# Attention and two MLPs with Strassen products: three weight steps a batch in attention, VectorE's queue filled up to TensorE's clock, and two output chunks in turns at two borders

## The chip, the cores and the metric

The kernel runs on one core of one Trainium2 chip. The metric is the device time of one execution in microseconds; the time before is the median of three runs. The profile is one further execution, recorded by the hardware profiler; its times count from the start of the recorded span.

## The reference

Three stages follow each other. Everything is fp32, on 896 tokens (2 batches of 448), 12 heads of 64, and a width of 768.

```python
scores = scale * np.matmul(q, k.transpose(0, 1, 3, 2)) - np.log(S)
attn = 1.0 / (1.0 + np.exp(-scores))
x = np.matmul(attn, v)                  # -> (896, 768)
# first MLP: 768 -> 1536 -> 768
rms = np.sqrt(np.mean(x * x, axis=-1, keepdims=True) + 1e-06)
xn = x / rms * rms_g
g = xn @ w_gate
x = g * (1.0 / (1.0 + np.exp(-g))) * (xn @ w_val) @ w_out
# second MLP: 768 -> 2048 -> 768
h = x @ w_in
out = h * (1.0 / (1.0 + np.exp(-h))) @ w_out2
```

## The kernel before

**Precision.** A product in fp32 is made of three passes on TensorE: each operand is split into a high part, rounded by ScalarE (`high`, L109), and a low part, the difference, taken by VectorE (`low`, L112); high by high, high by low and low by high are summed in PSUM. One matmul is 128x128 by 448 columns.

**Weights.** All weights come as 68 slabs of 128x768. Each goes through two raw buffers, three float tiles and a ring of four split tiles. The halves are these: `front` (Prelu on ScalarE L122, a shift on VectorE L125, a combining step on VectorE L127, and then the next slab's load, L106, on the queue of SP), and `back_std` (high, then low) or, for a Strassen product, `back_mac` (four more sums on VectorE, and four pairs of high and low). `step()` advances this stream by one instruction or two. So a slab's load is issued only when the slab two ahead of it has been combined at L127, and the loads of keys (`load_pair`, L378) and values are on the same queue, in program order.

**Order.** Nothing reorders: every engine runs its instructions as the program wrote them. What is written when is set by a small planner: `clock["pe"]` and `clock["dve"]` sum up costs of TensorE and VectorE as the code goes, and after each piece of TensorE's work `pump()` calls `step()` as long as VectorE's clock stays half a microsecond (`MARGIN`) below TensorE's. A second list, `fore`, holds sums and splits of activations, which takes turns with the weights. A product that needs a weight tile that isn't there yet calls `step()` until it is.

**Stages.** Attention works on 12 pairs of heads in chunks of 112 rows, three chunks a batch (48 chunks, 16 batches): the scores of a batch (L407, ScalarE's sigmoid L415), then the value products of the batch before (L423). After each batch two weight steps are taken, while the batch before was of the pairs 1 to 6 (L539 to L543). The keys of pair i are split by VectorE (`prep`, L392) when pair i-1 starts. After attention come the opening products (L553 to L567): two gate chunks and two value chunks (g and v) of batch 0, while batch 1 is normalised, then the same for batch 1 (L615), then the value products v of p = 1 and, for p = 1 to 5, `strassen` g1 to g5 with a value product between. Each `strassen` (L302) is seven groups of nine matmuls on three PSUM banks (x, y, z), named A11, S1, S2, A12, S3, S4, A22 after their weights; ScalarE saves three of the partial results, VectorE adds three, ScalarE ends with silu (L344 to L348). The o stage multiplies the hidden vector h by the output weights, six chunks of 12 tiles; the i stage is one plain product and the seven strassens i1 to i7 with the result g, and the e stage multiplies g by the last weights, six chunks of 16 tiles, with a copy on VectorE (L742) and a store for each chunk. Before e the eight tiles of g are split (ghi by ScalarE, glo by VectorE, each in two halves of 896); these are the `fore` work of i7 and of the first e chunk.

Of the kernel before, what the change touches and what calls it, by code (L numbers as in the profile page):

```python
# [8 lines left out]
F32 = mybir.dt.float32  # L9
F32R = mybir.dt.float32r  # L10
U32 = mybir.dt.uint32
I32 = mybir.dt.int32
AF = mybir.ActivationFunctionType
# [3 lines left out]
B, H, S, D = 2, 12, 448, 64  # L17
NP = H // 2
DM = H * D
FF1, FF2 = 1536, 2048  # L20
P = 128
CP = 112
NC = S // CP
KD, K1, K2 = DM // P, FF1 // P, FF2 // P
SLAB = 6 * P
HALF = 3 * P
NT = B * S
EPS = 1e-6
BATCH = 3
MARGIN = 0.5  # L30
RING = 4
PASSES = ((0, 0), (0, 1), (1, 0))
ORDER = (0, 2, 4, 1, 3, 5)
# [3 lines left out]
def tile_attention_two_mlps(  # L37
# [27 lines left out]
    nc = tc.nc  # L65
# [7 lines left out]
    rp = ctx.enter_context(tc.tile_pool(name="rp", bufs=1))  # L73
# [13 lines left out]
    for p in range(1, K1 // 2):  # L87
        pair = [("mac", 4 * p), ("std", 4 * p + 2), ("std", 4 * p + 3)]
        items += pair if p > 1 else pair[1:] + pair[:1]
    first = 2 * K1  # L90
# [7 lines left out]
    order = [t for kind, s in items for t in ((s, s + 1) if kind == "mac" else (s,))]  # L98
# [9 lines left out]
    def high(dst, src):  # L108
        nc.scalar.activation(dst, src, AF.Copy)  # L109

    def low(dst, src, hi):
        nc.vector.tensor_tensor(dst, src, hi.bitcast(F32), ALU.subtract)  # L112
# [118 lines left out]
    fore, turn = [], [True]  # L231
    clock = {"pe": 0.0, "dve": 0.0}

    def step():

        if head[0] is None:
            head[0] = next(steps, StopIteration)
        can = head[0] is not None and head[0] is not StopIteration
        if fore and not (can and turn[0]):
            turn[0] = True  # L240
            cost, do = fore.pop(0)
            clock["dve"] += cost
            do()
            return True
        turn[0] = False
        if not can:
            return False
        clock["dve"] += head[0]
        head[0] = next(steps, StopIteration)
        return True  # L250

    def pump():
        clock["dve"] = max(clock["dve"], clock["pe"] - 3.0)
        while True:
            ahead = [c for c in (fore[0][0] if fore else None, head[0]) if c not in (None, StopIteration)]
            if ahead and clock["dve"] + min(ahead) > clock["pe"] - MARGIN:
                return
            if not step():
                return

    def evac(cost):
        clock["dve"] = max(clock["dve"], clock["pe"]) + cost

    def until(ready):
        while not ready():
            assert step()

    def weights(s):
        until(lambda: s in wt)
        return wt[s]  # L270

    def done(s, n=1):
        live["ring"] -= n
        del wt[s]


    def product(ps, tiles, acts, bs, last=True, after=None):

        n = len(tiles)
        ps = ps if isinstance(ps, list) else [ps[:, b, :S] for b in range(2)]  # L280
        for i, (w, a) in enumerate(zip(tiles, acts)):
            s, o = divmod(w, 6)
            until(lambda: a in act)
            t, x = weights(s)[:, :, o * P : (o + 1) * P], act[a]
            for step_, (jw, jx) in enumerate(PASSES):
                for b in bs:
                    nc.tensor.matmul(  # L287
                        ps[b],
                        t[:, jw],
                        x(jx)[:, b * S : (b + 1) * S],  # L290
                        start=(i == 0 and step_ == 0),
                        stop=(i == n - 1 and step_ == 2),
                    )
            clock["pe"] += 0.2027 * 3 * len(bs)
            if last and o == 5:
                done(s)
            if after:
                after(i)
            if not lead:
                pump()  # L300

    def strassen(name, s, forms, dst, after=None):  # L302

# [54 lines left out]
    act = {("x", k): (lambda j, k=k: x[k][:, j]) for k in range(KD)}  # L358
# [4 lines left out]
    with ExitStack() as actx:  # L363
# [10 lines left out]
        def load_pair(i):  # L374
            b, hp = pairs[i]
            kq[i] = ap.tile([P, 2, S], F32, tag="kq", name=f"kq{i}", bufs=3)
            if i:
                nc.sync.dma_start(kq[i], kqd[b, hp])  # L378
            else:
                for j in range(2):  # L380
                    nc.sync.dma_start(kq[i][:, j], kqd[b, hp, :, j])
# [122 lines left out]
        n = len(pairs)  # L504
# [12 lines left out]
        seen, ready = 0, []  # L517
        chunks = [(i, c) for i in range(n) for c in range(NC)]
        batches = [chunks[j : j + BATCH] for j in range(0, len(chunks), BATCH)]
        for before, batch in zip([[]] + batches, batches + [[]]):  # L520
            for i, c in batch:
                if c == 0:
                    if i + 1 < n:
                        prep(i + 1)
                    if i + 2 < n:
                        load_pair(i + 2)
                        load_v(i + 2)
                    if i == 0:
                        load_next()
                    if i == 2:  # L530
                        load_next()
                scores(i, c)
            while ready:
                collect(ready.pop(0))
            for i, c in before:
                attend(i, c)
                if c == NC - 1:
                    ready.append(i)
            for _ in range(2):  # L539
                if 0 < seen <= NP:  # L540
                    step()
                if seen > NP:
                    next(normal, None)  # L543
            seen = batch[-1][0] if batch else n
# [17 lines left out]
        r = npool.tile([P, S], F32, tag="r", name="r1")  # L562
# [8 lines left out]
    fp = ctx.enter_context(tc.tile_pool(name="fp", bufs=1, reuse_waits="tile"))  # L571

    def sums_of(name, r, t):

        (b11, b21), (b12, b22) = [[r[:, b, j] for j in range(2)] for b in range(2)]
        tt = nc.vector.tensor_tensor
        todo = [
            (0.62, lambda: tt(b11, b12, b11, ALU.subtract)),
            (0.62, lambda: tt(b12, b22, b12, ALU.subtract)),
            (0.62, lambda: tt(b22, b22, b11, ALU.subtract)),  # L580
            (0.62, lambda: tt(b21, b21, b22, ALU.subtract)),
        ]
        return todo
# [29 lines left out]
    f = [fp.tile([P, 2, NT], F32, tag=f"F{p}", name=f"h{p}") for p in range(K1 // 2)]  # L613
    xs6 = [("x", k) for k in ORDER]
    for n in range(4):  # L615
        product(opening[n], range(6 * n, 6 * n + 6), xs6, (1,))
        m = n % 2
# [32 lines left out]
    for p in range(1, NP1):  # L650
        final = p == NP1 - 1
# [6 lines left out]
        for m in range(2):  # L658
            ps = ps_tile(f"v{p}_{m}")
            s = 4 * p + 2 + m  # L660

            def after(i):
                if final and m == 1 and i in (1, 3):
                    free = [f"x{ORDER[j]}" for j in (i - 1, i)]
                    fore.extend(halve("h", 3 + i // 2, f[3 + i // 2], xp, free[0], xp, free[1]))
# [12 lines left out]
    w0 = 6 * 2 * K1  # L678
    x2 = {}
    r2 = [rp.tile([P, 2, 2, S], F32, tag=f"r{t}", name=f"yr{t}") for t in range(3)]  # L680
    for m in range(KD):
        ps = ps_tile(f"o{m}")

        def after(i):
            if m == KD - 1 and i in (3, 7):
                fore.extend(halves_of("y", r2[i // 4], i // 4))

        product(ps, range(w0, w0 + K1), [("h", k) for k in range(K1)], (0, 1), after=after)
        w0 += K1
        x2[m] = fp.tile([P, 2, NT], F32R, tag=f"F{m}", name=f"y{m}")  # L690
        v = x2[m].rearrange("p j (b s) -> p j b s", b=2)
        high(v[:, 0], ps[:, :, :S])
        low(v[:, 1], ps[:, :, :S], v[:, 0])
        evac(1.09)
        nc.scalar.activation(r2[m // 2][:, :, m % 2], ps[:, :, :S], AF.Copy)
        act["y", m] = lambda j, m=m: x2[m][:, j]
        if m % 2:
            fore.extend(sums_of("y", r2[m // 2], m // 2))
    fore.extend(halves_of("y", r2[2], 2))


# [8 lines left out]
    for p in range(NP2):  # L710
        pool, tag = (xp, f"x{p}") if p < 6 else (rp, f"r{p - 6}")
# [3 lines left out]
        s = w0 // 6  # L715
        if p == 0:
            for m in range(2):
                ps = ps_tile(f"i{m}")
# [14 lines left out]
    for q, (ht, lt) in enumerate(((0, 1), (2, 3)), 6):  # L733
        fore.extend(halve("g", q, g2[q], xp, f"x{ht}", xp, f"x{lt}"))

    for m in range(KD):
        for bs in ((0, 1),) if m < KD - 1 else ((0,), (1,)):
            ps = ps_tile(f"e{m}_{bs[0]}")
            product(ps, range(w0, w0 + K2), [("g", k) for k in range(K2)], bs, bs[-1] == 1)
            sl = slice(bs[0], bs[-1] + 1)  # L740
            o = rp.tile([P, 2, S], F32, tag=f"r{(2, 0, 1)[m % 3]}" if m < 5 else f"r{(1, 2)[bs[0]]}", name=f"out{m}_{bs[0]}")
            nc.vector.tensor_copy(o[:, sl], ps[:, sl, :S])  # L742
            evac(1.09)
            nc.sync.dma_start(out[m * P : (m + 1) * P, sl], o[:, sl])
        w0 += K2


def _slabs(w, nk, order=None):

    import numpy as np  # L750

    k, m = w.shape
    t = np.ascontiguousarray(w).view(np.int64).reshape(nk, P, m // P, P)
    t = t.transpose(2, 0, 1, 3)
    return t if order is None else t[:, list(order)]
# [36 lines left out]
```

## Time and profile before

| what | value |
|---|---|
| three runs | 599.11, 602.41, 605.66 us, median 602.41 |
| profiled execution | 599.66 us, its span 597.9 us |
| mean granted clock of TensorE in it | 0.982 of full speed |
| TensorE busy | 564.7 us, 94% of the span |
| VectorE busy | 350.0 us, 59% |
| ScalarE busy | 277.8 us, 46% |

The span is what the profile shows between first and last instruction; 1.76 us of the profiled execution lie around it. TensorE is busy nearly throughout, so time is lost or gained where it stands still or runs at the lower clock.

### The profile page before, as it was taken

What the parts mean: (1) busy time and instruction counts of PE and PEld (TensorE: products, weight loads), DVE (VectorE), ACT (ScalarE), POOL (GpSimd) and SP (SyncE); (2) the same over time, 40 slices, a digit from 0 to 9 for tenths busy, and PEclk for the clock granted to TensorE, in tenths of its full rate; (3) what the DMA queues carried; (4) which work ended last, traced back from release to release, by engine and by line L of the source; (5) the groups of instructions that cost most, each with busy time, mean ns of one, the idle gap of its engine ahead of it and who ended that gap; (6) DMA issues with size and microseconds to landing.
All of it is one profiled execution on the core that took longest, in us unless ns stands there. A gap on an engine that the chain in (4) does not pass through costs nothing.

```text
span 597.9 us, 7040 instructions
## 1 busy us (share of the span) xinstructions
PE 564.7 (94%) x2840; PEld 484.6 (81%) x2840; DVE 350.0 (59%) x503; ACT 277.8 (46%) x366; POOL 0.2 (0%) x4
## 2 busy tenths in 40 slices
PE   6999994999899999999999999998888979999997
PEld 4545564998799999999999999987777758999996
DVE  3557649496577674696444566666665794434200
ACT  5887834444345362664333445455456672222100
POOL 0000000000000000000000000000000000000000
PEclk9999996999899999999999999999898999999999
DMA  8645002141144342343333313313331244432000
GB/s 254 231 146 188 6 0 97 62 148 64 53 159 160 129 148 93 106 159 106 127 111 116 116 61 106 105 54 105 104 107 53 103 162 137 165 130 84 31 32 31
DMA packets 14512, 64.99 MB, mean 109 GB/s; under 512 B 1872, under 2 KB 2384, under 8 KB 14480
## 3 DMA queue, kind: packets, MB, share of 16 engines
q1 hardware_dynamic: 14480, 64.55, 32.7%
q8 instruction: 22, 0.36, 0.3%
q14 instruction: 10, 0.08, 0.0%
HBM read 61.79 MB, written 2.75 MB: 108 GB/s over the span
## 4 chain that ended last, share of the span: by engine, by line
PE 89%; DVE 7%; ACT 2%; DMA 0%; issue 0%; SPq 0%; DVEq 0%; ACTq 0%
PE e L287 17%; PE v L287 15%; PE o L287 15%; PE av L423 6%; PE sc L407 6%; PE g L287 3%; PE i L287 2%; DVE glo L112 2%; DVE w L112 2%; PE g2x L312 1%; PE i5x L312 1%; PE g4x L312 1%; PE i2x L312 1%; PE i1x L312 1%; PE g3x L312 1%; PE g5x L312 1%
## 5 line engine op out<-in xcount | busy, mean ns | idle before, releaser
L112 DVE TENSOR_TENSOR w<-f,w 128x768 fp32r<-128x768 f32 (+1 forms) x80 | 70.7, 894 | 109.3 <-ACT w L109 109.3
L109 ACT ACTIVATE w<-f 128x768 fp32r<-128x768 f32 (+1 forms) x80 | 63.0, 793 | 125.4 <-PE e L287 56.5
L287 PE MATMUL v<-x,w 128*128 128x448 f32 x432 | 91.4, 373 | 8.0 <-DVE w L112 8.0
L287 PE MATMUL e<-ghi,w 128*128 128x448 f32 x384 | 96.4, 366 | 0.0
L287 PEld LDWEIGHTS v<-x,w 128*128 128x128 f32 x432 | 83.1, 193 | 15.4 <-DVE w L112 8.4
L287 PEld LDWEIGHTS e<-ghi,w 128*128 128x128 f32 x384 | 72.1, 188 | 6.0 <-DVE w L112 0.4
L127 DVE SCALAR_TENSOR_TENSOR f<-f,raw 128x768 uint32<-128x768 uint32 x68 | 64.9, 955 | 13.7 <-ACT f L122 10.6
L122 ACT ACTIVATE f<-raw 128x768 f32<-128x768 f32 x68 | 61.4, 904 | 21.5 <-DMA raw<-in_w 17.2
L287 PE MATMUL o<-hhi,w 128*128 128x448 f32 x288 | 70.3, 366 | 0.0
L287 PE MATMUL e<-glo,w 128*128 128x448 f32 x192 | 58.1, 370 | 5.9 <-DVE glo L112 5.9
L287 PEld LDWEIGHTS o<-hhi,w 128*128 128x128 f32 x288 | 54.1, 188 | 4.2
L415 ACT ACTIVATE a<-sc,logs 112x896 f32<-112x896 f32 x48 | 45.0, 1004 | 10.4 <-PE sc L407 10.0
L287 PEld LDWEIGHTS e<-glo,w 128*128 128x128 f32 x192 | 35.4, 188 | 11.8 <-DVE glo L112 9.3
L287 PE MATMUL o<-hlo,w 128*128 128x448 f32 x144 | 40.9, 366 | 0.0
L407 PEld LDWEIGHTS sc<-ks 64*112 64x112 f32 x288 | 26.0, 184 | 17.7 <-ACT ks L396 4.5
L407 PE MATMUL sc<-ks 64*112 64x448 f32 x288 | 35.9, 394 | 4.5 <-ACT ks L396 4.5
L423 PE MATMUL av<-a,vr 112*64 112x448 f32 x192 | 39.6, 548 | 0.0
L125 DVE TENSOR_SCALAR raw<-raw 128x768 uint32<-128x768 uint32 x68 | 37.7, 554 | 2.4 <-DMA raw<-in_w 2.4
L423 PEld LDWEIGHTS av<-a,vr 112*64 112x64 f32 x192 | 12.4, 136 | 20.4 <-issue 18.3
L287 PEld LDWEIGHTS o<-hlo,w 128*128 128x128 f32 x144 | 27.1, 188 | 2.1
L742 DVE COPY out<-e 128x896 f32<-128x896 f32 (+1 forms) x7 | 6.7, 956 | 28.5 <-PE e L287 28.5
L112 DVE TENSOR_TENSOR glo<-g,ghi 128x896 fp32r<-128x896 f32 x16 | 17.0, 1082 | 3.8 <-ACT ghi L109 3.8
(252 smaller groups left out, 681.3 us busy)
## 6 DMA issues: line engine op xcount, KB each, us to landing
raw<-in_w SPq DMA_DIRECT2D x68, 768.0 KB, 4.3
kq<-in_kq SPq DMA_DIRECT2D x11, 448.0 KB, 6.4
vr<-in_v SPq DMA_DIRECT2D x12, 224.0 KB, 5.4
out_t<-out SPq DMA_DIRECT2D x5, 448.0 KB, 2.5
kq<-in_kq SPq DMA_DIRECT2D x2, 224.0 KB, 2.7
out_t<-out SPq DMA_DIRECT2D x2, 224.0 KB, 1.9
eye<-in_eye SPq DMA_DIRECT2D x1, 49.0 KB, 6.4
g_sb<-in_g SPq DMA_DIRECT2D x1, 3.0 KB, 6.6
```

What stands on the lines that cost most here:

```text
L109: nc.scalar.activation(dst, src, AF.Copy)
L112: nc.vector.tensor_tensor(dst, src, hi.bitcast(F32), ALU.subtract)
L122: nc.scalar.activation(f, words[:, :, 1].bitcast(F32), AF.Prelu, scale=2.0**-112, alpha=2.0**32)
L125: nc.vector.tensor_scalar(z, z, 29, None, ALU.logical_shift_right)
L127: nc.vector.scalar_tensor_tensor(fu, fu, 3, z, ALU.logical_shift_left, ALU.bitwise_or)
L287: nc.tensor.matmul(ps[b], t[:, jw], x(jx)[:, b * S : (b + 1) * S], start=(i == 0 and step_ == 0), stop=(i == n - 1 and step_ == 2),)
L312: nc.tensor.matmul(ps, w[a][:, jw, t * P : (t + 1) * P], forms(b, t, jx), start=(start and t == 0 and n == 0), stop=(stop and t == 2 and n ...
L407: nc.tensor.matmul(ps[:CP, h, :S], ks[i][rows, jk, 0, c * CP : (c + 1) * CP], ks[i][rows, jq, 1, :], start=(step == 0), stop=(step == 2),)
L415: nc.scalar.activation(a, ps[:CP, :, :S], AF.Sigmoid, bias=logs[:CP], scale=D**-0.5)
L423: nc.tensor.matmul(ps[h * D : (h + 1) * D], vr[i][:, c, h, :], a[:, h, :], start=(c == 0), stop=(c == NC - 1),)
L742: nc.vector.tensor_copy(o[:, sl], ps[:, sl, :S])
```

## The change

There are three parts. `pump()` loses its half microsecond: steps are now written as long as VectorE's clock stays at or below TensorE's. In attention three weight steps are taken after a batch in place of two (while the batch before was of pair 6, two). And a new function `duo` runs the first two output chunks of o and of e in turns, two weight tiles (two k) for chunk 0 and then two for chunk 1, the second chunk in two single PSUM banks; the host lays the weight tiles out in that order. The results of these two chunks are taken out after both, in halves of 448 columns for each batch where they were 896 (`collected` for o, `put` for e).

```diff
-            if ahead and clock["dve"] + min(ahead) > clock["pe"] - MARGIN:
+            if ahead and clock["dve"] + min(ahead) > clock["pe"]:
...
-    def product(ps, tiles, acts, bs, last=True, after=None):
+    def product(ps, tiles, acts, bs, last=True, after=None, first=True, final=True):
...
-                        start=(i == 0 and step_ == 0),
-                        stop=(i == n - 1 and step_ == 2),
+                        start=(first and i == 0 and step_ == 0),
+                        stop=(final and i == n - 1 and step_ == 2),
...
+    def duo(name, w, nk, key):
+
+        pair = [ps_tile(f"{name}0"), [bank(f"{name}1_{b}") for b in range(2)]]
+        for k in range(0, nk, 2):
+            for ps in pair:
+                product(ps, (w, w + 1), [(key, k), (key, k + 1)], (0, 1), first=k == 0, final=k == nk - 2)
+                w += 2
+        return [[pair[0][:, b, :S] for b in range(2)], pair[1]]
...
-            for _ in range(2):
-                if 0 < seen <= NP:
+            for j in range(3):
+                if 0 < seen <= NP - (j > 1):
                     step()
+                if j > 1:
+                    break
...
+    pair = duo("o", w0, K1, "h")
+    w0 += 2 * K1
+    for m in range(2):
+        collected(m, pair[m], [(slice(b, b + 1), pair[m][b].rearrange("p (a s) -> p a s", a=1)) for b in range(2)])
+    for m in range(2, KD):
...
+    pair = duo("e", w0, K2, "g")
+    w0 += 2 * K2
+    for m in range(2):
+        for b in range(2):
+            put(m, b, 1, pair[m][b].rearrange("p (a s) -> p a s", a=1))
+    for m in range(2, KD):
```

How instructions move is seen at three places. In the rows, the line comes first, then the operation, and out<-in; lines of the kernel after are its own.

The first is SP's queue in attention, before. `raw3` is the load of weight slab 3 (the slabs are used in the order 0, 1, 2, 3, 6, 7, 4), `kq6` the load of the keys and queries of pair 6, `vr6` its values.

```order
L385 DMA vr5_300<-in_v 112x512
L378 DMA kq6_354<-in_kq 128x896
L385 DMA vr6_356<-in_v 112x512
L106 DMA raw3_389<-in_w 128x1536
L378 DMA kq7_412<-in_kq 128x896
L385 DMA vr7_414<-in_v 112x512
L378 DMA kq8_479<-in_kq 128x896
L385 DMA vr8_481<-in_v 112x512
L106 DMA raw6_521<-in_w 128x1536
L378 DMA kq9_537<-in_kq 128x896
L385 DMA vr9_539<-in_v 112x512
```

And after:

```order
L393 DMA vr5_303<-in_v 112x512
L105 DMA raw3_344<-in_w 128x1536
L386 DMA kq6_360<-in_kq 128x896
L393 DMA vr6_362<-in_v 112x512
L386 DMA kq7_418<-in_kq 128x896
L393 DMA vr7_420<-in_v 112x512
L105 DMA raw6_439<-in_w 128x1536
L105 DMA raw7_486<-in_w 128x1536
L386 DMA kq8_491<-in_kq 128x896
L393 DMA vr8_493<-in_v 112x512
L386 DMA kq9_549<-in_kq 128x896
```

The load of raw3 now stands ahead of kq6 and not ahead of kq7, raw6 and raw7 stand ahead of kq8 (and, below the rows printed, raw4 ahead of kq10).

The second is VectorE's queue behind the normalisation of batch 1 (the opening products), before. `x4` and `x5` are the last normalised tiles, `w2` and `w3` split weights, `f3` a float tile; L578 is a sum of activations for the first strassen.

```order
L112 TENSOR_TENSOR x5_89<-xr2_92,x5_89 128x448
L112 TENSOR_TENSOR w2_570<-f2_432,w2_570 128x768
L127 SCALAR_TENSOR_TENSOR f3_523<-f3_523,raw3_389 128x768
L125 TENSOR_SCALAR raw6_521<-raw6_521 128x768
L112 TENSOR_TENSOR w3_982<-f3_523,w3_982 128x768
L578 TENSOR_TENSOR xr0_90<-xr0_90 128x448
L127 SCALAR_TENSOR_TENSOR f6_980<-f6_980,raw6_521 128x768
```

And after, where L588 is the same sum:

```order
L111 TENSOR_TENSOR x5_89<-xr2_92,x5_89 128x448
L588 TENSOR_TENSOR xr0_90<-xr0_90 128x448
L589 TENSOR_TENSOR xr0_90<-xr0_90 128x448
L124 TENSOR_SCALAR raw7_486<-raw7_486 128x768
L590 TENSOR_TENSOR xr0_90<-xr0_90 128x448
L591 TENSOR_TENSOR xr0_90<-xr0_90 128x448
L126 SCALAR_TENSOR_TENSOR f7_1035<-f7_1035,raw7_486 128x768
L111 TENSOR_TENSOR w6_1050<-f6_532,w6_1050 128x768
```

The steps of w2, f3 and w3 are no longer there (they stand in attention), and the sums and w6 follow the normalisation at once.

The third is ScalarE's queue at the border from strassen i2 to i3, before. L332 is the last save of i2, L344 to L348 its silu, `w42_0` to `w42_3` are the weight tiles of i3.

```order
L332 ACTIVATE i2s2_3007<-i2x_3002 128x448
L109 ACTIVATE w42_0_3067<-f42_2885 128x768
L344 ACTIVATE g2_2_3001<-g2_2_3001 128x448
L347 ACTIVATE g2_2_3001<-g2_2_3001 128x896
L348 ACTIVATE g2_2_3001<-i2x_3002 128x448
L109 ACTIVATE w42_1_3112<-s42_3050 128x768
L109 ACTIVATE w42_2_3114<-f43_3022 128x768
L109 ACTIVATE w42_3_3117<-f42_2885 128x384
```

And after, where L340 is the save and L352 to L356 are the silu:

```order
L108 ACTIVATE w42_0_3064<-f42_2892 128x768
L340 ACTIVATE i2s2_3018<-i2x_3013 128x448
L108 ACTIVATE w42_1_3079<-s42_3047 128x768
L108 ACTIVATE w42_2_3091<-f43_3029 128x768
L352 ACTIVATE g2_2_3012<-g2_2_3012 128x448
L108 ACTIVATE w42_3_3115<-f42_2892 128x384
L355 ACTIVATE g2_2_3012<-g2_2_3012 128x896
L356 ACTIVATE g2_2_3012<-i2x_3013 128x448
```

The high parts of w42_1, w42_2 and w42_3 now stand ahead of the last silu, where they stood behind it.

## Rows read from the trace of the kernel before

**Rows 1.** This is the trace split into stretches, core 0: from and to (us from the span's start), length, then for each engine the time it was busy and (in brackets) its number of instructions, then PEclk, the clock that TensorE was granted as a share of full speed, the share of the DMA engines in use, and GB/s. In order the stretches are attention, the opening products, the strassen of g1 and its border with g2, the strassen and products up to the o stage, the o stage with the first product of the i stage, the seven strassens i1 to i7, the first output chunk of the e stage as far as VectorE paces it, and the rest of the e stage.

```profile
4.50:79.80 75.30, 75.27 (x491) 39.57 (x491) 45.92 (x77) 58.48 (x72) 0.00 (x0) 1.00 0.48 155
79.80:136.00 56.20, 48.20 (x229) 43.86 (x228) 40.62 (x72) 22.62 (x30) 0.00 (x0) 0.91 0.25 85
136.00:167.20 31.20, 27.59 (x127) 24.82 (x126) 17.23 (x26) 12.80 (x19) 0.00 (x0) 0.95 0.16 51
167.20:264.10 96.90, 96.90 (x478) 89.61 (x478) 67.54 (x92) 48.87 (x66) 0.00 (x0) 1.00 0.41 139
264.10:366.20 102.10, 102.10 (x505) 94.71 (x505) 62.10 (x80) 43.23 (x52) 0.00 (x0) 1.00 0.31 102
366.20:469.00 102.80, 95.23 (x443) 84.83 (x442) 60.47 (x92) 53.58 (x80) 0.00 (x0) 0.97 0.27 91
469.00:494.70 25.70, 19.83 (x86) 15.10 (x85) 25.70 (x31) 21.36 (x26) 0.00 (x0) 1.00 0.45 154
494.70:594.30 99.60, 99.57 (x490) 92.06 (x490) 29.17 (x35) 14.85 (x18) 0.00 (x0) 1.00 0.27 89
```

**Rows 2.** This is the chain of work that ended last, whole span, in order of time: start (us), length (us), engine, tile, line and number of instructions.

```profile
97.34 9.44 PE v L287 x34
...
135.96 1.82 PE g1x L312 x9
...
153.00 2.52 PE g2x L312 x7
...
155.52 2.55 PE g2y L312 x9
...
167.19 14.59 PE v L287 x72
...
264.09 87.56 PE o L287 x432
...
366.24 1.82 PE i1x L312 x9
...
392.36 0.74 ACT w L109
...
393.12 0.97 DVE w L112
...
394.13 1.69 PE i3y L312 x7
...
424.51 2.85 PE i5y L312 x9
...
489.47 2.00 DVE glo L112 x2
...
491.47 0.47 DVE raw L125
...
491.94 0.87 DVE w L112
...
494.73 99.59 PE e L287 x490
...
594.34 0.62 DVE out L742
```

**Rows 3.** This is the same chain in a stretch of attention: one batch of three score chunks (sc) and the three value products (av) one batch behind.

```profile
68.72 2.01 PE sc L407 x18
70.73 2.41 PE av L423 x12
73.14 2.03 PE sc L407 x18
```

**Rows 4.** This is the timeline of the queue of SP, which issues the loads of the first third: start, length, line and the load issued.

```profile
22.17 0.43 SPq L378 DMA_DIRECT2D kq<-in_kq  x1
...
33.57 0.33 SPq L106 DMA_DIRECT2D raw<-in_w  x1
...
33.95 0.42 SPq L378 DMA_DIRECT2D kq<-in_kq  x1
...
34.94 0.70 SPq L378 DMA_DIRECT2D kq<-in_kq  x1
```

**Rows 5.** This is the timeline of VectorE in attention: start, length, line, operation, and in square brackets the idle time ahead of it and what ended it.

```profile
26.77 0.63 DVE L442 TENSOR_TENSOR acc<-acc,sq 128x448 f32<-128x448 f32 x1 [4.34 <-ACT sq L441]
...
32.54 0.95 DVE L127 SCALAR_TENSOR_TENSOR f<-f,raw 128x768 uint32<-128x768 uint32 x1
...
41.78 0.62 DVE L392 CAST ks<-kq 128x896 fp32r<-128x896 f32 x1
...
44.76 0.63 DVE L442 TENSOR_TENSOR acc<-acc,sq 128x448 f32<-128x448 f32 x1 [0.70 <-ACT sq L441]
...
52.59 0.63 DVE L392 CAST ks<-kq 128x896 fp32r<-128x896 f32 x1 [2.04 <-DMA kq<-in_kq]
```

**Rows 6.** This is the page's part on DMA issues, the key loads: number, KB each, and the median time from issue to landing (us).

```profile
kq<-in_kq SPq DMA_DIRECT2D x11, 448.0 KB, 6.4
```

**Rows 7.** This is the waits of TensorE, whole span: who waited for whom, us in total, times, longest us.

```profile
PE v L287 <- DVE w L112: 8.0, 1, 8.0
...
PE e L287 <- DVE glo L112: 5.9, 7, 1.5
```

**Rows 8.** This is the timeline in the last strassen, i7: TensorE's second group on the bank i7x (S2).

```profile
463.24 2.09 PE L312 MATMUL i7x<-y,w 128*128 128x448 f32 x9 [0.69 <-ACT i7s L332]
```

More of the change, by code (lines that the diff above doesn't have):

```diff
@@ L29 @@
 BATCH = 3
-MARGIN = 0.5
 RING = 4
@@ L680, in tile_attention_two_mlps, with collected @@
     r2 = [rp.tile([P, 2, 2, S], F32, tag=f"r{t}", name=f"yr{t}") for t in range(3)]
-    for m in range(KD):
+    def collected(m, ps, views):
+        if m not in x2:
+            x2[m] = fp.tile([P, 2, NT], F32R, tag=f"F{m}", name=f"y{m}")
+        for sl, src in views:
+            h, l = (x2[m][:, j].rearrange("p (b s) -> p b s", b=2)[:, sl] for j in range(2))
+            high(h, src)
+            low(l, src, h)
+            evac(1.09 if sl == slice(0, 2) else 0.62)
+            nc.scalar.activation(r2[m // 2][:, sl, m % 2], src, AF.Copy)
+        act["y", m] = lambda j, m=m: x2[m][:, j]
+        if m % 2:
+            fore.extend(sums_of("y", r2[m // 2], m // 2))
+    both = slice(0, 2)
+    pair = duo("o", w0, K1, "h")
[3 more added lines that the diff above has]
+    for m in range(2, KD):
         ps = ps_tile(f"o{m}")
@@ L689, in tile_attention_two_mlps @@
         w0 += K1
[L690 to L698, printed above, removed]
+        collected(m, ps, [(both, ps[:, :, :S])])
     fore.extend(halves_of("y", r2[2], 2))
@@ L734, in tile_attention_two_mlps, with put @@
         fore.extend(halve("g", q, g2[q], xp, f"x{ht}", xp, f"x{lt}"))
-    for m in range(KD):
+    def put(m, b, n, src):
+        o = rp.tile([P, n, S], F32, tag=f"r{(2 * m + b) % 3}", name=f"out{m}_{b}")
+        nc.vector.tensor_copy(o, src)
+        evac(0.13 + 0.48 * n)
+        nc.sync.dma_start(out[m * P : (m + 1) * P, b : b + n], o)
+    pair = duo("e", w0, K2, "g")
[4 more added lines that the diff above has]
+    for m in range(2, KD):
         for bs in ((0, 1),) if m < KD - 1 else ((0,), (1,)):
@@ L739, in tile_attention_two_mlps @@
             product(ps, range(w0, w0 + K2), [("g", k) for k in range(K2)], bs, bs[-1] == 1)
[L740 to L744, printed above, removed]
+            put(m, bs[0], len(bs), ps[:, bs[0] : bs[-1] + 1, :S])
         w0 += K2
@@ L770 @@
     for name, nk, order in (("moe_w_out", K1, None), ("moe2_w_in", KD, ORDER), ("moe2_w_out", K2, None)):
-        tiles.append(_slabs(inputs[name], nk, order).reshape(-1, P, P))
+        t = _slabs(inputs[name], nk, order)
+        if order is None:
+            duo = t[:2].reshape(2, nk // 2, 2, P, P).transpose(1, 0, 2, 3, 4).reshape(2, nk, P, P)
+            t = np.concatenate([duo, t[2:]])
+        tiles.append(t.reshape(-1, P, P))
     w = np.concatenate(tiles)
```

## The prediction

> **What bounds the kernel now.** I read the stretches first, then the chain, then the waits. TensorE is busy for the whole length of attention, of the stretch from 167.2 to 264.1, of the o stage and of the last hundred microseconds [rows 1]. There a matmul costs 87.56 / 432 = 0.2027 us in the o stage [rows 2], at a granted clock of 1.00 (2.4 GHz), and no other engine can make these stretches shorter. Four stretches are left where TensorE's busy time is well under the length: the opening products (48.20 of 56.20), g1 with its border to g2 (27.59 of 31.20), i1 to i7 (95.23 of 102.80) and the first e chunk (19.83 of 25.70); in the first three the clock, too, is under 1.00 [rows 1]. The chain says who holds TensorE up there: low parts of weights on VectorE and, ahead of them, high parts on ScalarE [rows 2]. So the question for each part is whether the awaited step now comes earlier, and what then comes last.
>
> **Opening products (third step in attention).** Before, the value product stands still for 8.0 us, on the low part of a weight tile [rows 7]: w2 stands on VectorE behind the whole normalisation of batch 1. When TensorE goes on, its clock is low: 34 matmuls take 9.44 us where 34 x 0.2027 = 6.89, and from 97.34 to 135.96, the start of g1, 38.62 us pass for 34 + 36 + 108 matmuls that cost 36.08 [rows 2]. After the change w2 and w3 are split in attention, in the place where the order shows them gone from behind the normalisation. The two value products of batch 0 are then 72 x 0.2027 = 14.6 us of work that covers the normalisation, and the wait and the low clock go together: 8.0 + 2.54 = **-10.5**. If another tile (w6, which now follows the first sums) were late, the wait could come back in part; it has those 14.6 us and the 29 us of the second halves ahead of it, so I take the whole, with 8 as the lower end.
>
> **Attention itself.** A batch takes 2.01 + 2.41 = 4.42 us on TensorE [rows 3], and five more instructions of the weights on VectorE and two on ScalarE are put into it, with VectorE busy 45.92 and ScalarE 58.48 of 75.30 us [rows 1]. There is room on average. The risk is SP's queue. A raw load waits for the combining step two slabs back (L127), and everything behind it waits too. Before, kq6 is issued at 22.17, with nothing ahead of it; the raw load that now stands there needs the combining step of slab 1. That step moves up by one batch, from 32.54 to behind the sum at 26.77 [rows 5]: 26.77 + 0.63, a low part 0.87 and the step itself 0.87 give 29.1, with ScalarE's extra high part some 30. So kq6 is issued near 30.3, eight late, and lands after 6.4 [rows 6] at 36.7. The last batch, number 15, starts at 73.14 [rows 3]; counted back by 4.42 a batch, and by 1.8 for the two small products of the normalisation that lie between, batch 8, in which pair 6 begins, starts near 40.2, so that is covered. The second case is VectorE: a low part and the combining step of slab 3 now stand ahead of the split of pair 7 (before at 41.78 [rows 5]), and it ends about 1.2 after its first scores could start. The third is kq8, behind raw6 and raw7: issued near 45.4 (before 34.94 [rows 4]), landed at 51.8, split (0.62 and some 1.0) at 53.4; its scores are the third chunk of batch 10, counted back in the same way 50.4, plus the 1.2 lost already, 51.6. At the median landing it is 1.8 late, on a quick one in time. Together **+2.8**, with 0 (all of it covered) and 8 (kq8 and kq10 each a few microseconds late) as ends.
>
> **g1 and its border to g2 (the margin).** From 135.96 to 167.19 pass 31.23 us [rows 2] for 14 groups of nine matmuls, 126 x 0.2027 = 25.54; 5.69 is lost. The wait is on g2's second tile behind the gating of the first value products, and then g2 starts at the low clock: 7 matmuls 2.52, 9 matmuls 2.55 [rows 2]. Without the margin the steps of g2's tiles are written ahead of the evacuations of g1's end. I take **-5.3**, keeping 0.4 for the next tile, which is still close. Where weight steps stand ahead of an evacuation, it is the evacuation that comes late; g3 to g5, which have no gap now, get a shift (0.47 [rows 2]) or a low part (0.87) ahead of the add that their last group waits for. At some 0.4 for each of the three that is **+1.2** (ends 0 and 3 x 0.87 = 2.6).
>
> **i1 to i7 (the margin).** 102.80 us [rows 1] stand against 49 x 9 x 0.2027 = 89.39. At each border the second group waits for a high part (0.74 from 392.36) and a low part (0.97 from 393.12), behind the last silu, and goes on at 394.13; after some borders TensorE is slow as well, as in i5y, 2.85 for nine [rows 2]. The order shows the three high parts ahead of the last silu. The saves and adds of the strassen at work then have these 0.74 each ahead of them, but each has more than one group (1.82) until its bank is wanted again. The tightest place is i7, where splits of g join the queue of ScalarE: there S2 already waits 0.69 for a save [rows 8], and I put a wait of 0.8 in. Together 13.4 - 0.9 = **-12.5** (ends 9 and 13.4).
>
> **First chunks of o and e (the turns).** In o nothing waits now (102.10 of 102.10 busy, VectorE 62 [rows 1]), so the turns and the four narrower evacuations change **0**; the cover is the 14.6 us of the next chunk. In e, 125.34 us from 469.0 to 594.34 stand against 576 x 0.2027 = 116.76. VectorE is the bound there: two glo 2.00, a shift 0.47, a low part 0.87 and a combining step of the same width are 4.21 us for a pair of g tiles [rows 2], while TensorE is through with a pair in 12 x 0.2027 = 2.43. In turns the pair serves two chunks, 4.87 us. That is more than 4.21, so VectorE, which has the first glo done in i7, stays ahead: **-8.6** (lower end 6). The single banks of chunk 1 were read by i7's last silu, 2.4 us before they are written. The tail, a copy of 0.62 and a store, is as it was.
>
> **Sum.** -10.5 + 2.8 - 5.3 + 1.2 - 12.5 - 8.6 = -32.9. The profiled execution is 599.66, so 566.8; the median of the runs lies 2.75 above that execution, and I put 1.2 of it on top: **568**.
>
> **Rivals.** *A gain stays away:* weight steps ahead of evacuations give the gap back at a PSUM bank in i1 to i7, or VectorE still paces e. That is 568 + 8.6 = 577 or 568 + 12.5 = 580.5. For it speaks that ScalarE and VectorE work in order; against it, that both are busy only 53.58 and 60.47 of 102.80 us [rows 1]. *Attention loses three or four times as much* (late keys as above, for three pairs): 574 to 588. *Slower:* late keys all along. Five pairs now have their keys right behind a raw load. If each is needed as soon as before, and each comes later by the shift of kq6, 30.3 - 22.2 = 8.1, with TensorE at the low clock behind it (2.55 as at 97.34), that is 5 x 10.7 = 53 in place of 2.8: 618. It decides from (32.9 + 2.8) / 10.7, between three and four pairs. For it speaks that keys issued early already make VectorE wait 2.04 at 52.59 [rows 5]; against it, that kq6 has ten microseconds of cover and kq7 no new load ahead of it. *The change doesn't do what it says:* the order shows that it does for the weight steps; if the waits were on transfers and not on the steps, 599 to 603.
>
> Where chunks run in turns, TensorE changes banks every twelve matmuls. The strassens of 167.2 to 264.1 do that every nine, with three banks, at a clock of 1.00 and without a gap [rows 1]. If the turns were to bring the clock down all the same, the 336 matmuls of the two pairs of chunks would cost 2.52 / 7 - 0.2027 = 0.157 more each [rows 2], 53 us: 621. The Trainium skill (TensorE: Matmul & The Clock Gate, "A second HAM failure mode: psum-queue depth-cycling") tells of a kernel whose cycling through banks in each iteration let TensorE idle so often that its clock swung between the levels. The trace does not show that here for back-to-back groups.
>
> **How the numbers follow.** Chances: forecast 0.62, a gain stays away 0.20, attention dearer 0.10, slower by keys 0.04, by the clock in turns 0.01, no effect 0.03. The best case (every lost microsecond back, attention free) is 599.66 - 10.5 - 5.7 - 13.4 - 8.6 = 561.5; with a microsecond or so for runs against the profile the range starts at 560. It ends at 584, past the one-gain-missing cases and in the middle of the attention case. About 1% is what a measurement of this kernel can tell from no change: faster 0.92, same 0.03, slower 0.05.
>
> **What would show it.** Right: the wait of v on a low part is gone and the clock of the opening is near 1.00; the seven i strassens take 90 to 91 us; e shows no wait on glo; attention ends two to four microseconds later. Wrong: waits of sc on key splits of many microseconds; adds or saves (L338, L332) as releasers of TensorE in i1 to i7; glo still in the chain at e.

## The result, and the profile after

The changed kernel takes 570.63 us (median; 568.95 to 571.5), the kernel before 601.68 in the same comparison. The ratio is 0.9475, with a 95% interval from 0.9416 to 0.9534: 5% faster. The profiled execution took 570.01 us with a span of 568.2, so 29.7 us of span are gone.

The first view is the trace of the kernel after in stretches, with the same columns and the same order of stages as in [rows 1]. Only the cut in e lies elsewhere: it stands where the first two chunks, in turns, end.

```profile
4.50:82.10 77.60, 76.06 (x491) 38.01 (x491) 49.99 (x82) 59.68 (x74) 0.00 (x0) 1.00 0.52 171
82.10:127.70 45.60, 45.60 (x229) 41.92 (x228) 37.97 (x68) 20.77 (x28) 0.00 (x0) 1.00 0.22 70
127.70:154.30 26.60, 25.85 (x128) 23.63 (x127) 19.20 (x29) 13.73 (x21) 0.00 (x0) 1.00 0.26 90
154.30:253.00 98.70, 97.48 (x478) 89.36 (x478) 64.63 (x88) 47.21 (x65) 0.00 (x0) 1.00 0.39 129
253.00:355.10 102.10, 102.10 (x505) 94.61 (x505) 62.00 (x82) 43.58 (x56) 0.00 (x0) 1.00 0.30 101
355.10:445.80 90.70, 89.90 (x443) 82.80 (x442) 66.10 (x99) 59.23 (x87) 0.00 (x0) 1.00 0.35 121
445.80:484.70 38.90, 38.90 (x190) 35.33 (x189) 27.64 (x33) 21.33 (x26) 0.00 (x0) 1.00 0.42 142
484.70:564.80 80.10, 80.09 (x388) 72.40 (x386) 21.37 (x28) 9.88 (x12) 0.00 (x0) 1.00 0.22 71
```

TensorE is busy over the whole of the opening (45.60 of 45.60, before 48.20 of 56.20), and in i1 to i7 over 89.90 of 90.70; no stretch shows a granted clock under 1.00. The second view is the chain that ended last, which answers [rows 2].

```profile
91.25 7.31 PE v L286 x36
...
127.73 1.82 PE g1x L320 x9
...
142.48 0.96 DVE w L111
...
143.48 1.69 PE g2y L320 x7
...
154.29 14.59 PE v L286 x72
...
252.99 87.55 PE o L286 x432
...
355.13 1.82 PE i1x L320 x9
...
435.62 0.54 ACT i7s L335
...
436.19 2.12 PE i7x L320 x9
...
438.32 1.86 PE i7z L320 x9
...
445.76 119.05 PE e L286 x576
...
564.83 0.62 DVE out L760
```

The value product now follows the gate products at once (91.25). The waits left in the chain are one on a low part at g2 (142.48), one in i7 on ScalarE's save (435.62), and short ones in attention and in g3 to g5, below. The e stage is one unbroken row of 576 matmuls, 119.05 us. By stage, from the first matmul of each in the chain:

| stage | before | after | difference | predicted |
|---|---|---|---|---|
| attention, to the first g | 79.83 | 82.14 | +2.31 | +2.8 |
| opening, to g1 | 56.13 | 45.59 | -10.54 | -10.5 |
| g1 and g2 | 31.23 | 26.56 | -4.67 | -5.3 |
| g3 to g5 with their products | 96.90 | 98.70 | +1.80 | +1.2 |
| o and first product of i | 102.15 | 102.14 | -0.01 | 0 |
| i1 to i7 | 102.74 | 90.63 | -12.11 | -12.5 |
| e, to the last copy | 125.36 | 119.07 | -6.29 | -8.6 |
| last copy and store | 3.56 | 3.37 | -0.19 | 0 |
| sum | 597.9 | 568.2 | -29.70 | -32.9 |

Attention lost a little more than its row says: TensorE got through its first scores 0.83 us faster (5.89 us to 10.44, before 6.74 to 11.27), which has nothing to do with the change, so some 3.1 were lost behind them. Two views show where. The first is SP's queue after (as in [rows 4]):

```profile
28.64 0.33 SPq L105 DMA_DIRECT2D raw<-in_w  x1
...
29.01 0.43 SPq L386 DMA_DIRECT2D kq<-in_kq  x1
...
44.50 0.42 SPq L386 DMA_DIRECT2D kq<-in_kq  x1
```

The raw load is issued at 28.64 and the keys of pair 6 right behind it, at 29.01 (before 22.17); kq8 comes at 44.50 (before 34.94). The second is TensorE's timeline, its matmuls (PE) and weight loads (PEld), with the idle time and its end in brackets:

```profile
45.77 1.28 PE L415 MATMUL sc<-ks 64*112 64x448 f32 x10 [0.58 <-DVE ks L401]
...
49.43 2.84 PE L415 MATMUL sc<-ks 64*112 64x448 f32 x18
...
50.32 0.48 PEld L415 LDWEIGHTS sc<-ks 64*112 64x112 f32 x6 [0.42 <-ACT a L423]
...
51.21 0.17 PEld L415 LDWEIGHTS sc<-ks 64*112 64x112 f32 x2 [0.41 <-ACT a L423]
...
51.60 0.27 PEld L415 LDWEIGHTS sc<-ks 64*112 64x112 f32 x4 [0.21 <-DVE ks L401]
...
60.31 0.97 PE L431 MATMUL av<-a,vr 112*64 112x448 f32 x4 [0.86 <-DVE xr L443]
```

The split of pair 7 is 0.58 late. The scores from 49.43 take 2.84 us in this view, where 2.1 is usual: their second and third chunk each start about 0.3 late, behind ScalarE's sigmoids (L423), which have weight steps ahead of them, and some 0.2 more goes to the split of pair 8, whose scores are the third chunk. At 60.31 a value product waits for VectorE's copy (L443) of an earlier one.

### The profile page after: what moved, and what is told of

The parts are those of the page before. It is cut to its first block, busy times and chain, and to the rows that moved or that the text cites. A ratio compares the mean times of both kernels' runs of the same rounds, so it can differ in the third digit from the quotient of the medians.

```text
span 568.2 us, 7054 instructions
## 1 busy us (share of the span) xinstructions
PE 556.0 (98%) x2840; PEld 478.1 (84%) x2840; DVE 350.2 (62%) x507; ACT 277.5 (49%) x370; POOL 0.2 (0%) x4
## 4 chain that ended last, share of the span: by engine, by line
PE 87%; DVE 5%; ACT 3%; DMA 2%; issue 1%; SPq 0%; DVEq 0%; ACTq 0%
PE e L286 21%; PE v L286 15%; PE o L286 15%; PE av L431 4%; PE sc L415 4%; PE g L286 3%; PE i L286 3%; DMA kq<-in_kq 2%; PE i5x L320 1%; PE i6x L320 1%; PE i4x L320 1%; PE i2x L320 1%; PE i1x L320 1%; PE i3x L320 1%; PE i7x L320 1%
## 5 line engine op out<-in xcount | busy, mean ns | idle before, releaser
L286 PE MATMUL e<-ghi,w 128*128 128x448 f32 x384 | 97.6, 368 | 0.0
L286 PE MATMUL v<-x,w 128*128 128x448 f32 x432 | 88.9, 366 | 0.0
L286 PEld LDWEIGHTS v<-x,w 128*128 128x128 f32 x432 | 81.1, 188 | 6.8 <-issue 0.4
L423 ACT ACTIVATE a<-sc,logs 112x896 f32<-112x896 f32 x48 | 44.8, 1007 | 5.7 <-PE sc L415 5.6
L415 PEld LDWEIGHTS sc<-ks 64*112 64x112 f32 x288 | 24.5, 178 | 20.7 <-ACT a L423 8.5
L760 DVE COPY out<-e 128x448 f32<-128x448 f32 (+1 forms) x9 | 6.8, 776 | 31.9 <-PE e L286 27.8
```

What stands on the lines that cost most here:

```text
L286: nc.tensor.matmul(ps[b], t[:, jw], x(jx)[:, b * S : (b + 1) * S], start=(first and i == 0 and step_ == 0), stop=(final and i == n - 1 and ...
L415: nc.tensor.matmul(ps[:CP, h, :S], ks[i][rows, jk, 0, c * CP : (c + 1) * CP], ks[i][rows, jq, 1, :], start=(step == 0), stop=(step == 2),)
L423: nc.scalar.activation(a, ps[:CP, :, :S], AF.Sigmoid, bias=logs[:CP], scale=D**-0.5)
L760: nc.vector.tensor_copy(o, src)
```

## The experiments

The theory is the sum of the prediction: each part of the change works on its own stage. The rivals make one part do the work of another, or put a loss elsewhere. The first four runs take the parts away one at a time.

**Two steps again.** The loop in attention goes back:

```diff
-            for j in range(3):
-                if 0 < seen <= NP - (j > 1):
+            for _ in range(2):
+                if 0 < seen <= NP:
                     step()
```

> The changed kernel with two weight steps a batch in attention again; margin gone and chunks in turns as in the change. Theory (the third step alone buys the opening): the wait of the value product on the low part of w2 comes back with its low clock, +10.5 us, and attention gets back the 3 us it lost; 570 + 7.5 = about 578. Rival (the opening runs through because the margin is gone, and the third step only costs): 567 to 568, and no wait of v on a low part.

Measured: 578.17 us (ratio to the kernel before 0.9597, 0.9551 to 0.9644). The opening takes 56.30 us again and attention, counted from its first score, 75.62 (changed kernel 77.57); all other stages are within 0.5 us of the changed kernel. TensorE's timeline has the old wait and the slow matmuls behind it, 9.61 us for 34:

```profile
97.70 9.61 PE L286 MATMUL v<-x,w 128*128 128x448 f32 x34 [8.00 <-DVE w L111]
```

So the third step alone buys the 10.5 us, and costs 2 to 3 in attention (the first scores of this run were 1.2 us slower than those of the changed kernel).

**The margin back.**

```diff
-            if ahead and clock["dve"] + min(ahead) > clock["pe"]:
+            if ahead and clock["dve"] + min(ahead) > clock["pe"] - 0.5:
```

> The changed kernel with the margin of half a microsecond back in the planner; three steps and turns stay. Theory (the margin alone makes the borders): the border g1 to g2 loses 4.7 us again, the waits inside g3 to g5 (1.8 us) go, the borders of i1 to i7 lose 12 us again: 570 + 15 = about 585, with waits of i3x to i7x on high and low parts of weights. Rival (the third step has put the whole stream of weights ahead, so that the margin matters little): 570 to 575.

Measured: 583.87 us (0.9702, 0.9657 to 0.9747). g1 and g2 take 31.24, g3 to g5 96.91 and i1 to i7 102.73, the lengths of the kernel before to within 0.01 us; the opening stays at 45.59. The border i3 to i4 shows both waits of before:

```profile
398.79 0.67 PE L320 MATMUL i4x<-y,w 128*128 128x448 f32 x2 [1.36 <-ACT w L108]
399.78 1.68 PE L320 MATMUL i4x<-y,w 128*128 128x448 f32 x7 [0.33 <-DVE w L111]
```

The e stage, however, takes 117.06, two less than in the changed kernel. That was not expected and led to the second part of the study.

**No turns.** The loops of o and e and the host's order are those of before; margin and third step are as in the change.

```diff
-    pair = duo("e", w0, K2, "g")
-    w0 += 2 * K2
...
-    for m in range(2, KD):
+    for m in range(KD):
```

> The changed kernel without the turns: the six chunks of o and of e run one after the other as before, with three steps and without margin. Theory (VectorE needs 4.2 us for a pair of g tiles and TensorE 2.43): e loses between 6.3 (what was gained) and 8.6 us, waits of e on glo are back: 576 to 579. Rival (without the margin the splits of g run so far ahead in i7 that e has little to wait for): 570 to 573.

Measured: 578.31 us (0.9606, 0.9549 to 0.9663). The e stage takes 125.44 and TensorE waits for the splits of g:

```profile
461.78 0.68 PE L287 MATMUL e<-glo,w 128*128 128x448 f32 x2 [0.86 <-DVE glo L112]
...
463.65 0.67 PE L287 MATMUL e<-glo,w 128*128 128x448 f32 x2 [0.38 <-DVE glo L112]
...
466.50 0.67 PE L287 MATMUL e<-ghi,w 128*128 128x448 f32 x2 [1.77 <-ACT ghi L109]
```

In all TensorE stands still for 3.8 us of this stage (125.44 less 121.61 busy), in the kernel before for 5.9. So the rival is right in part: there is less to wait for. The rest of the loss follows behind the waits: the granted clock is 0.58 from 467.66 to 471.76, and from there on the matmuls take 0.2067 us each in place of 0.2027, the slower of the two paces that the runs below are about. The turns are needed; that VectorE's queue runs ahead in i7 does not replace them.

**Turns in e alone.** The o stage is written as before.

```diff
-    pair = duo("o", w0, K1, "h")
-    w0 += 2 * K1
-    for m in range(2):
-        collected(m, pair[m], [...])
-    for m in range(2, KD):
+    for m in range(KD):
```

> The changed kernel with the chunks of o one after the other as before, turns in e alone. Theory (nothing waits at the border to o): the o stage takes 102.1 in both, 570. Rival (VectorE's splits of h, which without margin and with the third step come at another time, would hold up a single chunk): o longer by 1 to 3 us.

Measured: 570.46 us (0.9472, 0.9437 to 0.9508), the o stage with the first product of i 102.15. The turns in o do nothing.

**The margin back in g2 to g5 alone.**

```diff
+            keep[0] = 0.5
             strassen(f"g{p}", 4 * p, forms_of(x), f[p])
+            keep[0] = 0.0
```

where `pump()` compares with `clock["pe"] - keep[0]`.

> The changed kernel with the margin of half a microsecond back in the strassens g2 to g5 alone. Theory (weight steps written ahead of the adds make the waits of the last groups of g3, g4 and g5, 0.6 us each): these three waits go and nothing else changes, about 568. Rival (the waits come from the order of the weights and not from the margin): 570, the same waits.

Measured: 566.79 us (0.9429, 0.9379 to 0.948). In the changed kernel the last group of g3 waits for an add, as in this row of its timeline:

```profile
180.26 2.09 PE L320 MATMUL g3x<-t,w 128*128 128x448 f32 x9 [0.44 <-DVE h L346]
```

and those of g4 and g5 in the same way. With the margin these waits are no longer there; what stays is a tenth to a quarter of a microsecond in the last group (1.95 and 2.07 where a group takes 1.86 or 1.82), where only the weight load waits for the add. But the profiled execution was the slowest of the four, 571.05 (the others, of which there is no trace, 566.09 to 567.39), and its chain shows a difference of that size:

```profile
252.95 89.28 PE o L287 x432
...
357.11 1.86 PE i1x L321 x9
...
443.63 1.82 PE i7x L321 x9
...
449.10 116.75 PE e L287 x576
```

The o stage takes 89.28 us for 432 matmuls, 0.2067 each, where it was 87.55; a strassen group takes 1.86; and from the wait in i7 on it is 1.82 again, and e takes 116.75, which is 0.2027 for each of 576. So there are two paces of TensorE, 2% apart, both at a granted clock of 1.00. In the changed kernel the slow one sits behind the wait in i7: 1.86 for i7z at 438.32, and 119.05 / 576 = 0.2067 for e.

**The first save of i7 ahead.** ScalarE's save that the wait in i7 is for is written before the splits of g and the weight steps.

```diff
+            if save is not None:
+                nc.scalar.activation(saved[save], ps, AF.Copy)
             if after:
                 after(a)
             pump()
```

> The changed kernel; in the last strassen i7 alone, ScalarE's save of the first group is written ahead of the splits of g and the weight steps that stood before it. Theory 1 (a wait of TensorE can leave it at 0.2067 us a matmul, 2% slower, until its next wait; in the changed kernel that is the wait of i7 and then the whole of e): the wait of 0.8 goes, and with it the slow pace, e takes 117 instead of 119: 570 - 3 = 567. Theory 2 (the slow pace belongs to e as the change writes it, its splits and turns): only the 0.8 goes and e keeps 0.2067: 569.

Measured: 569.45 us (0.947, 0.9438 to 0.9502), a gain too small for the times alone. The trace, of the quickest execution (568.31; the others 568.75 to 571.23), shows two things. The wait did not go; it moved to the last group, where VectorE's add now stands behind a low part and a glo, and i1 to i7 take 91.04 instead of 90.63:

```profile
444.23 2.09 PE L320 MATMUL i7x<-y,w 128*128 128x448 f32 x9 [1.04 <-DVE g L350]
```

And behind that other wait e goes at the fast pace, with its splits and turns unchanged:

```profile
446.32 116.75 PE e L286 x576
```

That speaks against theory 2.

**Two waits added in e.** Ahead of the fourth and the fifth chunk VectorE sets a bank to zero, behind its copy of the chunk before.

```diff
             ps = ps_tile(f"e{m}_{bs[0]}")
+            if m in (3, 4):
+                nc.vector.memset(ps[:, 0, :S], 0.0)
```

> The changed kernel with two added waits: ahead of the fourth and the fifth output chunk of e VectorE sets the first bank to zero, behind its copy of the chunk before, so TensorE waits some 1.6 us twice. Nothing is left out. Theory (the pace of TensorE is settled anew by each wait and kept until the next): the matmuls before the first added wait go at 0.2067 us, and after one of the two or both at 0.2027, so the time is 570 + 3.2 less 0.8 to 1.5. Rival (the slow pace belongs to e): 0.2067 throughout, 573.

Measured once: 580.52 us, so the time was missed by far: the first wait is 5.07 us and not 1.6 (VectorE's copy, ahead of it, itself came late), the second 1.80, and the granted clock behind them is 0.51 (511.66 to 514.76) and 0.62 (534.55 to 539.04). On the pace the trace is plain. Two glo rows that lie six matmuls apart stand 1.24 us apart before the wait and 1.22 behind it:

```profile
503.12 0.57 PE L286 MATMUL e<-glo,w 128*128 128x448 f32 x2
...
504.36 0.57 PE L286 MATMUL e<-glo,w 128*128 128x448 f32 x2
...
511.66 1.08 PE L286 MATMUL e<-ghi,w 128*128 128x448 f32 x2 [5.07 <-DVE e L773]
```

```profile
519.62 0.57 PE L286 MATMUL e<-glo,w 128*128 128x448 f32 x2
...
520.84 0.56 PE L286 MATMUL e<-glo,w 128*128 128x448 f32 x2
```

That is 0.2067 and 0.203 us a matmul, in the same stage, with the same kind of work and a granted clock of 1.00 in both stretches. So the slow pace does not belong to e as the change writes it; the run without turns, which had it in e from 471.76 on, says the same from the other side.

**Keys sooner.** A fourth key buffer, and each key load one pair sooner.

```diff
-            kq[i] = ap.tile([P, 2, S], F32, tag="kq", name=f"kq{i}", bufs=3)
+            kq[i] = ap.tile([P, 2, S], F32, tag="kq", name=f"kq{i}", bufs=4)
...
-                    if i + 2 < n:
-                        load_pair(i + 2)
+                    if i + 3 < n:
+                        load_pair(i + 3)
```

> The changed kernel with a fourth buffer for keys, the load of the keys issued one pair sooner, so that kq8 stands ahead of the weight loads that it stood behind. Theory (the loss in attention is kq8 and its successors landing late): the wait of kq8's split is gone and attention takes 1.5 to 2.3 us less: 568 to 568.5. Rival (the loss is on VectorE and ScalarE, which take the weight steps ahead of splits, sums and sigmoids in their order): attention as in the changed kernel, 570.

Measured: 567.64 us (0.9438, 0.9409 to 0.9467). Attention takes 75.69 (changed kernel 77.57). The wait for pair 7 shrinks to 0.24, and the copy holds the value product up by little (2.84 us for its twelve matmuls, 2.48 where nothing is in the way; in the changed kernel 3.55 from 57.73 to the end of the row at 60.31):

```profile
44.98 1.27 PE L415 MATMUL sc<-ks 64*112 64x448 f32 x10 [0.24 <-DVE ks L401]
...
56.53 2.84 PE L431 MATMUL av<-a,vr 112*64 112x448 f32 x12
```

So 1.9 of some 3.1 us were the keys behind the weight loads. What stays speaks for the rival: the 0.24 is the split of pair 7 behind a low part and a combining step on VectorE, and the chunks that started behind ScalarE's sigmoids still do, as at 50.42:

```profile
50.42 0.48 PEld L415 LDWEIGHTS sc<-ks 64*112 64x112 f32 x6 [0.42 <-ACT a L423]
```

**The mends together.** First the margin in g2 to g5, the save and the keys.

> The changed kernel with the margin back in the strassens g2 to g5, the first save of i7 ahead, and the keys one pair sooner. Theory (the three add up): 570 - 1.8 - 3 - 1.5 = about 564, if no wait leaves TensorE at the slow pace. Rival (a slow pace after some other wait, 0.004 us a matmul, takes back what is won): 566 to 569.

Measured: 565.51 us (0.9403, 0.9378 to 0.9427), between the theory's 564 and the rival's range. The wait in the last group of i7 (1.02) is still there, as in the run with the save alone, and the slow pace shows from g2's second tile to the last group of g3 (14.88 us for the 72 matmuls of v from 152.68). Then a margin of 1.5 us in i7 as well:

```diff
+            keep[0] = 1.5 if p == NP2 - 1 else 0.0
             strassen(f"i{p}", s, forms_of(x2), g2[p], after)
+            keep[0] = 0.0
```

> The kernel with the three mends, and in i7 a margin of 1.5 us, so that VectorE's adds stand ahead of the further splits of g. Theory (the wait of the last group of i7, 1.02, is VectorE's low part and glo in front of the add): this wait goes, i7 takes 0.8 to 1.0 less, and e is not held up, since VectorE has 4.9 us for each pair of tiles and needs 4.2: 564.5. Rival (the splits put off come back as waits of e on glo): 565.5 to 568.

Measured: 564.72 us (0.9401, 0.936 to 0.9442; five of the six runs 563.91 to 564.94, one, of which there is no trace, 570.95). i1 to i7 take 89.37 us, the 49 x 9 x 0.2027 = 89.39 that the matmuls cost, and e 116.75:

```profile
352.59 1.82 PE i1x L321 x9
...
441.96 116.75 PE e L287 x576
...
558.74 0.62 DVE out L771
```

Against the three mends that is no difference that the times can tell, but against the changed kernel it is 5.9 us by the medians, with intervals that do not separate fully (0.936 to 0.9442 and 0.9416 to 0.9534); the profiled spans, 562.1 and 568.2, differ by as much.

## Why the prediction was right, point by point

**What bounds the kernel.** That TensorE is the bound held in every run: stretches without a gap kept their length to 0.01 us (o and the first product of i: 102.14 to 102.15). That time goes only where TensorE stands still or is granted the lower clock did not hold: in the one run that had the slow pace there the same stretch took 104.16, busy throughout at a granted clock of 1.00.

**Opening.** -10.54 against -10.5. Both terms, the 8.0 us of waiting and 2.5 of low clock, went together, and the run with two steps brought both back.

**Attention.** +2.31, or 3.1 without the faster start, against +2.8. Kq6 was put at 30.3 and issued at 29.01, kq8 at 45.4 and issued at 44.50. The landing of kq8 was counted at 6.4 and took 5.20, so its split ended at 51.55 and not at 53.4, and cost the scores 0.2 and not 1.8. Pair 7 was 0.58 late instead of 1.2. Two things were not in the sum: the 0.6 that two chunks of scores waited for ScalarE's sigmoids, and the wait of 0.86 at 60.31, where the copy of a value product stands on VectorE behind a late split and the normalisation. That the sum came out near is luck: its errors cancelled.

**g1 and g2, g3 to g5.** -4.67 against -5.3, because g2's second tile, where 0.4 was kept, costs 1.0: its low part lets TensorE stand still for 0.75, and the first weight load and matmul behind the wait are not hidden; and +1.80 against +1.2, because each of the three last groups lost 0.6 instead of 0.4 (0.4 of standing still and the same start behind it). The mechanism, an add behind weight steps on VectorE, is the one that the row at 180.26 names, and all but a quarter of a microsecond of it goes with the margin.

**i1 to i7.** -12.11 against -12.5. All borders are closed; the one wait left is in i7, on ScalarE's save, with 0.80 as put in. A save as releaser of TensorE was among the signs of being wrong, but this is the one that the sum had. The rest of the difference is the start behind that wait (0.2 to 0.3) and the slow pace after it (0.2).

**e.** -6.29 against -8.6. The step "in turns the pair serves two chunks, 4.87 us, more than 4.21" was right: no wait on glo is left. The term was mis-sized because every matmul was taken at 0.2027 and 576 of them went at 0.2067, 2.3 us in all. Where TensorE kept the fast pace the stage took 117.06 (margin back) or 116.78 (margin in g2 to g5, the save ahead, and both sets of mends), which is -8.3 to -8.6.

**Rivals.** None came true. (The upper end of the attention rival, 588, is not the four times 2.8 that it names, which gives 576; it is near three pairs that each come 8.1 late, 589.5.) The keys were late, but the cover that the prediction gave as the reason against (ten microseconds for kq6) held. The Trainium skill's rule (TensorE: Matmul & The Clock Gate, "A second HAM failure mode: psum-queue depth-cycling") did not show: in the 38.9 us of turns in e the granted clock was 1.00 and TensorE busy for all of it. The prediction's "changes banks every twelve matmuls" is loose: each product writes two banks, one for each batch, in turn, and it is this pair of banks that changes every twelve.

**The sum.** In the profiled execution 29.7 us are gone where the sum had 32.9. Of the 3.2 that are missing, 2.5 are the slow pace (2.3 in e, 0.2 in i7) and 1.2 lie in g1 to g5; i7's start behind its wait adds 0.2, and attention and the tail give 0.7 back. The 1.2 us put on top for the median were 0.6 (570.63 against 570.01), so the forecast of 568 lay 2.6 us under the median.

## What to carry to other kernels

Where engines run in a fixed order, ask of each wait of the bounding engine which instruction stands ahead of the awaited one; writing the next stage's weight steps ahead of the last evacuations can be worth the whole gap, and what is then late are the evacuations, so leave the margin out only where a border has a gap. A pair of output chunks in turns halves the rate at which freshly made operands are asked for, which pays where another engine makes them (e) and nothing where it keeps up (o). A prefetch step taken earlier also moves its load, and everything behind that load in the same queue: move the other loads ahead of it.

## What the runs showed of the hardware that was not expected

TensorE has two paces for the same back-to-back matmuls (128x128 by 448, fp32 passes, a weight load for each) at a granted clock of 1.00: 0.2027 and 0.2067 us, as in 87.55 and 89.28 us for the 432 of the o stage. By the starts of the matmuls in all twelve traces it changed only where the stream was broken: behind a wait of TensorE, in g3 and g4 behind one of its weight load alone, and in the opening behind the small products of the normalisation (the 18 gate matmuls of batch 0 that follow the eight products with `ones` go at 0.2067 in every run). It then stayed over hundreds of matmuls and over changes of stage: from 436 to the end in the changed kernel, from the last group of g4 to the wait in i7 in the run with the margin in g2 to g5, up to the added wait in the run with two of them. The same wait gave either pace: the 0.75 us on g2's second tile were followed by the fast one in the changed kernel and by the slow one, 14.88 for 72 matmuls of v, in the run with the margin in g2 to g5 and in the run with two waits added in e, whose program up to there is that of the changed kernel. So neither the program nor the length of the wait decides alone; what does is open, and no run chose the pace. A short wait can so be followed by a loss longer than itself: 2.5 us behind the 0.8 in i7 of the changed kernel, some 4.4 behind the weight load's wait of 0.33 in g4 of the run with the margin in g2 to g5.
